# Summing the squares of two pairs with identity matmuls in PSUM, and leaving out the slope clamp

## The chip, the cores and the metric

The kernel runs on one core of one Trainium2 chip. The metric is the device time of one execution in microseconds, the median of several; before the change it was 736.23 us, the median of three runs from 736.1 to 736.62. The core has a matrix engine (TensorE, PE in the profile, with its weight loads shown apart as PEld), a vector engine (VectorE, DVE), an engine for functions of one input (ScalarE, ACT), a general engine (GpSimd, POOL) and a queue that issues transfers (SyncE, SP). Each runs its own instructions in the order in which they stand in its stream, and waits on semaphores for the others.

## What is computed

A linear attention with a complex, token-wise decay, then a dense layer pair with a softplus, then four experts with a ReLU. Only the attention's decay matters here:

```python
mag = np.sqrt(a_re * a_re + a_im * a_im)
scale = np.minimum(mag, 0.999) / (mag + 1e-06)
a_re_n, a_im_n = (a_re * scale, a_im * scale)
for t in range(S):
    ar, ai = (a_re_n[:, :, t, :, None], a_im_n[:, :, t, :, None])
    new_re = ar * S_re - ai * S_im
    new_im = ar * S_im + ai * S_re
    S_re, S_im = (new_re + kv, new_im)
    y[:, :, t] = np.einsum('bhd,bhde->bhe', q[:, :, t], S_re)
```

There are 2 batches, 8 heads, 768 tokens a batch and 48 numbers a head. The magnitude of the decay needs the sum of two squares, its logarithm and a running sum over the tokens; its angle needs an arctangent and a running sum as well.

## The kernel before

The tokens lie on the 128 partitions, 128 at a time (a chunk, 128 by 384 numbers for 8 heads). Two chunks make a pair; pairs 0 to 2 are batch 0, pairs 3 to 5 batch 1. For each pair `front(n)` makes the decay: `squares` (L545 to L547) squares both parts on ACT into T1 and T2 and adds them into T2, on DVE for pair 0 and on GpSimd for all others. `ratio` (L550 to L556) takes T1 to 1/|re| with a logarithm and an exponential on ACT, and four operations on DVE make the argument of the arctangent in `im`; the last of them, L556, clamps it to plus or minus 1.5. `logmag` turns T2 into the logarithm of the magnitude. `prefix` adds the last row of the chunk before (L574, on GpSimd, one partition) and makes the running sum by a matmul with a triangle of ones; `wrap`, `level` and `carry` copy it out and send the last row on by a transfer. `trig` takes sine and cosine. Sine and arctangent need another function table on ACT than logarithm and exponential, so `excursion` loads one table, runs them and loads the first again (L97). `back(n)` is the attention of the two chunks: `decay` (L653), the product with queries and keys QK (L665), transposes `tp` (L674), scores `sp` (L683) with the mask on DVE (L684), the mixing `yps` (L699), the state `sps` (L710), and X, the input of the dense layers, split in a high and a low half.

The dense layers of batch 0 (k = 0 and 1) run in the same stretch. Their weights arrive as 64-bit numbers in halves: three DVE operations (L70 to L72) join a half into one of two buffers `f`, ACT and DVE split it in two (L181, L182), and a transfer stores it for batch 1 (`moe_weights`). `gemm1` (L232) makes h; `first` and `second` make g from h by ACT and DVE (Abs, Exp, Ln, L250, L275, L276), and `third` (L314) multiplies g with the second weights into y. For k = 0 the tokens come in three blocks of two chunks, and one `e` or `g` holds two of the eight slices of the hidden layer: g_0_1, g_0_3, g_0_5 and g_0_7 are block 0.

The units of all these parts are put in one list of events with a place each, and sorted. From that list each engine's stream is laid down when the kernel is built: an instruction stands where the builder, which keeps its own account of when operands are ready, found it ready and first in the list. On the chip each stream is then run in that order. PSUM buffers of tag "a" (three) are shared by the running sums, the scores and the state.

Of the kernel before, what the change touches and what calls it, by code (L numbers as in the profile page):

```python
# [9 lines left out]
F32 = mybir.dt.float32  # L10
# [4 lines left out]
AF = mybir.ActivationFunctionType  # L15
ALU = mybir.AluOpType
# [7 lines left out]
P = 128  # L24
B, H, S, D = 2, 8, 768, 48
HD = H * D
# [23 lines left out]
SLOPE_MAX = 1.5  # L50
# [25 lines left out]
def fast_path(ctx: ExitStack, tc, bad, wsc, qkv, a_re, a_im, w_in, w_out, probs, w1, w2, out):  # L76
    nc = tc.nc
# [8 lines left out]
    psum = ctx.enter_context(tc.tile_pool(name="psum", bufs=1, space=PSUM))  # L86
# [6 lines left out]
    def behind(ins, earlier):  # L93
        tc.add_manual_dep(ins.ins, earlier.ins.name, NOSYNC, reason="order on one engine")
# [7 lines left out]
    def act(out_, in_, fn, **kw):  # L102
        i = nc.scalar.activation(out_, in_, fn, **kw)  # L103
        if fn in (AF.Exp, AF.Ln, AF.Sin, AF.Arctan):
            behind(i, tabs["load"])
            tabs["since"].append(i)
        return i

    use_table(LOGEXP)
    ident = const.tile([P, P], F32, name="ident")  # L110
# [12 lines left out]
    def column(name, value):  # L123
        t = const.tile([P, 1], F32, name=name)
        nc.vector.memset(t, value)
        return t
# [4 lines left out]
    b_tiny = column("b_tiny", 1e-37)  # L131
# [387 lines left out]
            third(*pipe.pop(0))  # L519

    rows = [None]
    st_S = [None]
    st = {}

# [3 lines left out]
    def wide(t, sl):  # L528
        return flat(t[:, sl, :])
# [13 lines left out]
    def squares(n, sl):  # L543
        R, I, T1, T2 = (wide(t, sl) for t in st[n])
        nc.scalar.activation(T1, R, AF.Square)  # L545
        nc.scalar.activation(T2, I, AF.Square)
        (nc.vector if n == 0 else nc.gpsimd).tensor_tensor(T2, T1, T2, ALU.add)  # L547

    def ratio(n, sl):
        R, I, T1, T2 = (wide(t, sl) for t in st[n])  # L550
        act(T1, T1, AF.Ln, bias=b_tiny)
        act(T1, T1, AF.Exp, scale=-0.5)
        nc.vector.tensor_tensor(R, R, T1, ALU.mult)
        nc.vector.scalar_tensor_tensor(R, R, 2.0, T1, ALU.subtract, ALU.mult)
        nc.vector.tensor_tensor(I, I, R, ALU.mult)
        nc.vector.tensor_scalar(I, I, SLOPE_MAX, -SLOPE_MAX, ALU.min, ALU.max)  # L556

    def logmag(n, sl):
        T1, T2 = wide(st["z0"][1] if n == 0 else st[n][2], sl), wide(st[n][3], sl)
        act(T2, T2, AF.Ln, bias=b_tiny)  # L560
        act(T1, T2, AF.Exp, scale=-0.5)
        nc.vector.tensor_scalar(T2, T2, 0.5, LOG_CAP, ALU.mult, ALU.min)
        nc.vector.scalar_tensor_tensor(T2, T1, -1e-6, T2, ALU.mult, ALU.add)
# [173 lines left out]
    def front(n):  # L737
        return [lambda: s1_load(n), lambda: squares(n, both), lambda: ratio(n, both), excursion(lambda: arctan(n)),
                lambda: logmag(n, both)] + s2_units(n) + [excursion(lambda: trig(n))]
# [40 lines left out]
    level(0, 0)  # L780
    decay(0, 0)
    squares(1, both)
    ratio(1, both)
    level(0, 1)
# [314 lines left out]
@with_exitstack  # L1099
def attention_moe_kernel(ctx: ExitStack, tc, qkv, a_re, a_im, w_in, w_out, probs, w1, w2, v, out):  # L1100
    nc = tc.nc
    top = ctx.enter_context(tc.tile_pool(name="top", bufs=1))
    bad = top.tile([1, 1], I32, name="bad")
    wsc = nc.dram_tensor("moe1_weights", (16, P, 768), F32).ap()
    fast_path(tc, bad, wsc, qkv, a_re, a_im, w_in, w_out, probs, w1, w2, out)
    xs = nc.dram_tensor("attention_out", (NTOK, HD), F32).ap()
    flag = nc.values_load(bad[0:1, 0:1], min_val=0, max_val=1)
    with tc.If(flag > 0):
        general_path(tc, xs, v, qkv, a_re, a_im, w_in, w_out, probs, w1, w2, out)
# [53 lines left out]
```

## Time and profile before

| What | Value |
|---|---|
| Median of three runs | 736.23 us |
| Profiled execution, its span | 736.2 us (nothing of its time is shown outside the span) |
| PE busy | 703.0 us, 95% |
| DVE busy | 584.7 us, 79% |
| ACT busy | 487.0 us, 66% |
| POOL busy | 33.3 us, 5% |
| Granted TensorE clock, mean | 0.986 |

The shares are means over stages that differ. In the 40 slices of the profile's page (18.4 us each) PE stands at 1, 6, 8, 8 and then 9 tenths throughout, while DVE is at 9 from the second to the eighth slice and lower later on. So the stages are read apart: the first 91 us, in which the attention of batch 0 and the weights' conversion fill DVE and ACT, and the rest, in which PE works without a pause.

### The profile page before, as it was taken

What the parts mean: (1) busy time and instruction counts of PE and PEld (TensorE: products, weight loads), DVE (VectorE), ACT (ScalarE), POOL (GpSimd) and SP (SyncE); (2) the same over time, 40 slices, a digit from 0 to 9 for tenths busy, and PEclk for the clock granted to TensorE, in tenths of its full rate; (3) what the DMA queues carried; (4) which work ended last, traced back from release to release, by engine and by line L of the source; (5) the groups of instructions that cost most, each with busy time, mean ns of one, the idle gap of its engine ahead of it and who ended that gap; (6) DMA issues with size and microseconds to landing.
All of it is one profiled execution on the core that took longest, in us unless ns stands there. A gap on an engine that the chain in (4) does not pass through costs nothing.

```text
span 736.2 us, 13313 instructions
## 1 busy us (share of the span) xinstructions
PE 703.0 (95%) x5171; PEld 676.2 (92%) x5171; DVE 584.7 (79%) x1150; ACT 487.0 (66%) x898; POOL 33.3 (5%) x31
## 2 busy tenths in 40 slices
PE   1688999999999999999999999999999999999996
PEld 0477899999899999999999999999999999999996
DVE  6999999955875854648888779988788899988963
ACT  7887886878896856345686666555556667666640
POOL 1132010000111011000000000000000000000000
PEclk9699999999999999999999999999999999999998
DMA  7655666721211420121022130213454445554501
GB/s 264 195 175 170 230 190 195 228 84 44 75 55 59 122 81 2 59 86 44 23 86 65 29 102 21 87 44 98 128 159 146 137 151 172 151 172 140 172 32 69
DMA packets 36486, 83.56 MB, mean 113 GB/s; under 512 B 4544, under 2 KB 13376, under 8 KB 36416
## 3 DMA queue, kind: packets, MB, share of 16 engines
q1 hardware_dynamic: 36128, 82.35, 35.5%
q8 instruction: 42, 0.69, 0.4%
q10 hardware_dynamic: 288, 0.30, 0.1%
q14 instruction: 28, 0.23, 0.1%
HBM read 73.95 MB, written 8.65 MB: 112 GB/s over the span
## 4 chain that ended last, share of the span: by engine, by line
PE 70%; DVE 10%; DMA 9%; ACT 8%; issue 2%; POOL 1%; SPq 0%; ACTq 0%; POOLq 0%; DVEq 0%
PE y L314 21%; PE h L232 18%; PE z L314 9%; PE px L425 7%; PE pv L425 3%; PE tp L674 2%; DMA rawB<-in_w_dram 2%; DMA chkw<-in_w_in_dram 2%; PE pc L425 2%; PE sp L683 2%; PE yps L699 2%; DMA chki<-in_a_im_dram 1%; PE ya L359 1%; PE sps L710 1%; DVE fA L72 1%
## 5 line engine op out<-in xcount | busy, mean ns | idle before, releaser
L232 PE MATMUL h<-X,A 128*128 128x384 f32 (+1 forms) x936 | 176.1, 329 | 2.5 <-ACT A L181 0.8
L232 PEld LDWEIGHTS h<-X,A 128*128 128x128 f32 x936 | 153.4, 188 | 5.8 <-issue 1.6
L314 PE MATMUL y<-B,g 128*128 128x384 f32 x744 | 150.0, 335 | 0.0
L314 PEld LDWEIGHTS y<-B,g 128*128 128x128 f32 x744 | 131.1, 188 | 0.5 <-issue 0.2
L314 PE MATMUL y<-g,B 128*128 128x384 f32 (+1 forms) x504 | 91.0, 315 | 0.3 <-ACT g L285 0.3
L314 PE MATMUL z<-B,g 128*128 128x384 f32 x372 | 84.7, 334 | 0.0
L314 PEld LDWEIGHTS y<-g,B 128*128 128x128 f32 x504 | 79.3, 189 | 1.9 <-ACT g L285 0.6
L314 PEld LDWEIGHTS z<-B,g 128*128 128x128 f32 x372 | 66.3, 188 | 0.0
L247 ACT ACTIVATE e<-h 128x384 f32<-128x384 f32 (+1 forms) x60 | 30.8, 513 | 37.3 <-PE h L232 36.3
L250 DVE SCALAR_TENSOR_TENSOR e<-h,e 128x384 f32<-128x384 f32 (+1 forms) x60 | 34.9, 581 | 21.0 <-ACT e L103 20.1
L255 DVE SCALAR_TENSOR_TENSOR g<-h,g 128x384 fp32r<-128x384 f32 x32 | 17.7, 554 | 28.2 <-ACT g L254 28.2
L103 ACT ACTIVATE e<-e,b_one 128x384 f32<-128x384 f32 (+1 forms) x60 | 38.2, 637 | 1.3
L103 ACT ACTIVATE e<-e 128x384 f32<-128x384 f32 (+1 forms) x60 | 32.8, 547 | 1.3
L425 PE MATMUL px<-X,sA 128*128 128x384 f32 x144 | 33.7, 339 | 0.0
L425 PE MATMUL px<-XC,sA 128*128 128x384 f32 x144 | 33.0, 337 | 0.1
L314 PE MATMUL z<-g,B 128*128 128x384 f32 x144 | 32.9, 335 | 0.0
L674 PE MATMUL tp<-ident,QK 128*96 128x128 f32 x192 | 27.3, 290 | 5.9 <-DVE QK L665 5.0
L674 PEld LDWEIGHTS tp<-ident,QK 128*96 128x96 f32 x192 | 22.4, 133 | 10.0 <-DVE QK L665 6.2
L254 ACT ACTIVATE g<-h 128x384 fp32r<-128x384 f32 x32 | 15.6, 487 | 21.3 <-PE h L232 21.1
L286 DVE TENSOR_TENSOR g<-e,g 128x384 fp32r<-128x384 f32 x48 | 26.7, 555 | 3.8 <-ACT g L285 3.0
L490 ACT CAST B<-rawB 128x768 fp32r<-128x768 f32 x24 | 20.0, 835 | 14.1 <-DMA rawB<-in_w_dram 7.6
L490 ACT CAST A<-rawA 128x384 fp32r<-128x384 f32 (+1 forms) x48 | 20.3, 457 | 11.6 <-DMA rawA<-in_w_dram 9.2
(204 smaller groups left out, 1424.4 us busy)
## 6 DMA issues: line engine op xcount, KB each, us to landing
rawA<-in_w_dram SPq DMA_DIRECT2D x32, 384.0 KB, 3.0
rawB<-in_w_dram SPq DMA_DIRECT2D x32, 384.0 KB, 3.1
rawA<-in_w_in_dram SPq DMA_DIRECT2D x16, 384.0 KB, 3.7
rawB<-in_w_out_dram SPq DMA_DIRECT2D x16, 384.0 KB, 3.8
chkw<-in_w_in_dram SPq DMA_DIRECT2D x16, 384.0 KB, 3.5
chkw<-in_w_out_dram SPq DMA_DIRECT2D x16, 384.0 KB, 3.3
qk<-in_qkv_dram SPq DMA_DIRECT2D x12, 384.0 KB, 3.3
v<-in_qkv_dram SPq DMA_DIRECT2D x12, 256.0 KB, 3.1
```

What stands on the lines that cost most here:

```text
L103: i = nc.scalar.activation(out_, in_, fn, **kw)
L232: nc.tensor.matmul(ps, wt[:, p, kk, o:o + P], XB[b][:, q, kk, tok], start=(n == 0), stop=(n == 3 * KT - 1))
L247: nc.scalar.activation(t, h, AF.Abs)
L250: nc.vector.scalar_tensor_tensor(t, h, 0.0, t, ALU.max, ALU.add)
L254: nc.scalar.activation(g[:, 0, :], h, AF.Relu)
L255: nc.vector.scalar_tensor_tensor(g[:, 1, :], h, 0.0, g[:, 0, :].bitcast(F32), ALU.max, ALU.subtract)
L286: nc.vector.tensor_tensor(g[:, 1, :], t, g[:, 0, :].bitcast(F32), ALU.subtract)
L314: mm = nc.tensor.matmul(ys[j], l_, r_, start=(opens and n == 0 and not mate), stop=(closes and n == 2), skip_group_check=k == 0)
L425: nc.tensor.matmul(ps, lt[:, p, li, :], rhs, start=(start and n == 0), stop=(stop and n == 2), skip_group_check=True)
L490: nc.scalar.copy(hi, src)
L674: nc.tensor.transpose(tp[:96, hh, :], src[:, hf * 4 + hh, :], ident)
L683: nc.tensor.matmul(sp[:, hh, :], kT[:, hh, :], qT[:, hh, :], start=True, stop=True)
```

## The change

The squares of pairs 1 and 2 are no longer added by GpSimd. For each chunk of these pairs two matmuls with the identity as weights add T1 and T2 into a PSUM buffer, and ACT takes the logarithm from there into T2, so that `logmag` doesn't take it any more. Pairs 0, 3, 4 and 5 add as before. The clamp L556 is left out for all six pairs.

```diff
+    ON_PE = (1, 2)
...
-        (nc.vector if n == 0 else nc.gpsimd).tensor_tensor(T2, T1, T2, ALU.add)
+        if n not in ON_PE:
+            (nc.vector if n == 0 else nc.gpsimd).tensor_tensor(T2, T1, T2, ALU.add)
+            return
+        for c in range(2):
+            ps = psum.tile([P, 512], F32, tag="a", name=f"sq{n}_{c}", bufs=3)[:, :HD]
+            nc.tensor.matmul(ps, ident, st[n][2][:, c, :], start=True, stop=False)
+            nc.tensor.matmul(ps, ident, st[n][3][:, c, :], start=False, stop=True)
+            act(st[n][3][:, c, :], ps, AF.Ln, bias=b_tiny)
...
-        nc.vector.tensor_scalar(I, I, SLOPE_MAX, -SLOPE_MAX, ALU.min, ALU.max)
...
-        act(T2, T2, AF.Ln, bias=b_tiny)
+        if n not in ON_PE:
+            act(T2, T2, AF.Ln, bias=b_tiny)
```

The builder lays the streams down anew, and they move far more than the diff tells. Three places follow, all between 35 and 60 us of the trace of before. The numbers behind the names count buffers and differ between the two kernels; lines after the change are 8 higher from `ratio` on.

On PE, the end of the attention of pair 0's second chunk and the first matmuls of the dense layers, before and then now (`sps_1` is the state of that chunk, `sq` the new sums, of pair 2):

```order
L699 MATMUL yps_1_397<-A_1_1_390,v_1_140 32x128 x2
L710 MATMUL sps_1_440<-v_1_140,QK_1_325 32x64 x11
L232 MATMUL h_0_0_548<-X_119,A_0_351 128x256 x2
L232 MATMUL h_0_2_677<-X_119,A_1_501 128x256 x2
L232 MATMUL h_0_0_548<-X_119,A_0_351 128x256 x16
```

```order
L707 MATMUL yps_1_400<-A_1_1_393,v_1_140 32x128 x2
L718 MATMUL sps_1_443<-v_1_140,QK_1_328 32x64 x24
L553 MATMUL sq_0_503<-t_490,ident 128x384
L554 MATMUL sq_0_503<-t_491,ident 128x384
L553 MATMUL sq_1_507<-t_490,ident 128x384
L554 MATMUL sq_1_507<-t_491,ident 128x384
L232 MATMUL h_0_0_557<-X_119,A_0_354 128x256 x18
```

The sums of pair 2 stand behind the last matmul of pair 0's attention.

On ACT, the table load of the excursion with pair 1's sine and pair 2's arctangent, before and now (t_487 and t_490 are T1 of pair 2, `dec` is the decay of pair 1, with which its attention begins):

```order
L675 COPY qT_1_0_337<-tp_1_0_338 96x512
L103 ACTIVATE t_487<-t_487,b_tiny 128x768
L103 ACTIVATE t_487<-t_487 128x768
L721 CAST X_119<-yps_0_279 128x3x128
L181 CAST A_1_501<-fA_1_0_506 128x384
L675 COPY kT_1_0_344<-tp_1_0_345 96x512
L675 COPY qT_1_1_356<-tp_1_1_357 96x512
L97 ACT_TABLE_LOAD
L675 COPY kT_1_1_363<-tp_1_1_364 96x512
```

```order
L181 CAST A_2_630<-fA_2_0_645 128x384
L103 ACTIVATE t_491<-sq_0_503,b_tiny 128x384
L103 ACTIVATE t_490<-t_490,b_tiny 128x768
L103 ACTIVATE t_491<-sq_1_507,b_tiny 128x384
L103 ACTIVATE t_490<-t_490 128x768
L97 ACT_TABLE_LOAD
L103 ACTIVATE re_129<-re_129,b_hpi 128x768
L103 ACTIVATE im_130<-im_130 128x768
L247 ACTIVATE e_0_1_625<-h_0_0_557 128x512
L103 ACTIVATE im_489<-im_489 128x768
L97 ACT_TABLE_LOAD
L103 ACTIVATE dec_0_541<-t_132 128x384 x2
```

Pair 2's logarithm and exponential moved from ahead of the work on pair 0's second chunk to behind its last step, the copy X, which is the row ahead of these, and the table load moved with them.

On DVE, the start of pair 1's attention (`qk`, `QK`), before and now:

```order
L72 SCALAR_TENSOR_TENSOR fB_1_1_579<-rawB_1_1_542,fB_1_1_579 128x384
L653 SCALAR_TENSOR_TENSOR qk_0_224<-dec_0_532,qk_0_224 128x768
L182 TENSOR_TENSOR B_1_539<-fB_1_0_558,B_1_539 128x384
L665 TENSOR_TENSOR QK_0_536<-qk_0_224,re_129 128x16x48
L665 TENSOR_TENSOR QK_0_536<-qk_0_224,im_130 128x16x48
```

```order
L72 SCALAR_TENSOR_TENSOR fB_2_0_787<-rawB_2_0_745,fB_2_0_787 128x384
L561 TENSOR_TENSOR re_488<-re_488,t_490 128x768
L562 SCALAR_TENSOR_TENSOR re_488<-re_488,t_490 128x768
L563 TENSOR_TENSOR im_489<-im_489,re_488 128x768
L661 SCALAR_TENSOR_TENSOR qk_0_227<-dec_0_541,qk_0_227 128x768
L673 TENSOR_TENSOR QK_0_545<-qk_0_227,re_129 128x16x48
```

The weights of A_2 and the first half of B_2 now stand ahead of pair 1's attention, and behind pair 2's `ratio` the next instruction is the one that waits for `dec`.

## Rows read from the trace of the kernel before

**Rows 1.** Waits of PE after 140 us: line, releaser, total us, times, longest
```profile
PE pf L586 <- ACT hl L580: 0.4, 1, 0.4
PE y L314 <- ACT g L285: 0.3, 1, 0.3
```

**Rows 2.** Stretches: length, busy us of PE, PEld, DVE, ACT, POOL, clock, DMA, GB/s
```profile
41.00:58.00 17.00, 13.56 (x184) 11.16 (x183) 16.97 (x29) 16.02 (x28) 2.32 (x2) 1.00 0.56 165
58.00:92.00 34.00, 31.68 (x406) 27.51 (x405) 32.16 (x60) 27.30 (x49) 5.93 (x4) 1.00 0.61 200
92.00:150.00 58.00, 58.00 (x584) 55.83 (x583) 55.09 (x110) 45.40 (x91) 2.44 (x1) 1.00 0.63 201
150.00:280.00 130.00, 129.21 (x1017) 123.79 (x1017) 83.60 (x134) 101.04 (x171) 13.84 (x11) 1.00 0.23 71
```

**Rows 3.** Chain that ended last, 88 to 96 us: start, us on it, what
```profile
90.83 0.52 ACT g L275
...
91.39 0.50 PE y L314 x2
```

**Rows 4.** Timeline, pair 1's sum: start, us, engine, line [idle before <- releaser]
```profile
12.09 0.89 PE L593 MATMUL pl<-t,tri 128*128 128x384 f32 x2
...
12.44 2.09 POOL L547 TENSOR_TENSOR t<-t,t 128x768 f32<-128x768 f32 x1 [10.71 <-ACT t L546]
12.91 2.04 DVE L555 TENSOR_TENSOR im<-im,re 128x384 f32<-128x384 f32 x1
...
14.57 0.94 ACT L103 ACTIVATE t<-t,b_tiny 128x768 f32<-128x768 f32 x1 [1.02 <-POOL t L547]
...
19.54 1.65 PE L593 MATMUL pf<-im,trik 128*128 128x384 f32 x2 [6.55 <-ACT im L103]
```

**Rows 5.** The clamp's line, all of the run: duration ns min/median/max
```profile
L556 DVE TENSOR_SCALAR im<-im x7: 349/550/555, 12.1 to 255.4; 128x768 f32<-128x768 f32 x5, 128x384 f32<-128x384 f32 x2
```

**Rows 6.** Timeline, 37 to 59 us: pair 2's sum and the excursion
```profile
37.36 1.82 POOL L547 TENSOR_TENSOR t<-t,t 128x768 f32<-128x768 f32 x1 [3.04 <-ACT t L546]
...
38.57 1.03 DVE L72 SCALAR_TENSOR_TENSOR fA<-rawA,fA 128x384 int32<-128x384 int32 x1
...
39.22 0.94 ACT L103 ACTIVATE t<-t,b_tiny 128x768 f32<-128x768 f32 x1 [1.47 <-POOL t L547]
...
40.19 0.85 ACT L103 ACTIVATE t<-t 128x768 f32<-128x768 f32 x1
...
40.63 0.99 POOL L574 TENSOR_TENSOR t<-rows,t 1x384 f32<-1x384 f32 x1 [0.17 <-DMA rows<-t]
...
47.62 0.68 DVE L684 TENSOR_TENSOR A<-sp,tri 128x512 f32<-128x512 f32 x1
...
48.29 0.94 ACT L103 ACTIVATE re<-re,b_hpi 128x768 f32<-128x768 f32 x1
48.36 0.86 PE L699 MATMUL yps<-A,v 128*32 128x128 f32 x24 [0.41 <-DVE A L684]
...
51.08 1.28 ACT L97 ACT_TABLE_LOAD   x1
...
52.38 0.94 ACT L103 ACTIVATE dec<-t 128x384 f32<-128x384 f32 x2
...
58.33 0.95 DVE L563 SCALAR_TENSOR_TENSOR t<-t,t 128x768 f32<-128x768 f32 x1
```

**Rows 7.** Timeline of DVE, 92 to 95 us: successive starts give the pitch
```profile
92.85 0.95 DVE L665 TENSOR_TENSOR QK<-qk,im 128x768 f32<-128x768 f32 x1
93.72 0.56 DVE L71 SCALAR_TENSOR_TENSOR fA<-rawA,fA 128x384 int32<-128x384 int32 x1
94.19 0.69 DVE L250 SCALAR_TENSOR_TENSOR e<-h,e 128x512 f32<-128x512 f32 x1
94.79 0.55 DVE L72 SCALAR_TENSOR_TENSOR fA<-rawA,fA 128x384 int32<-128x384 int32 x1
```

**Rows 8.** Timeline, pair 2's second wrapped angle, which the second excursion waits for
```profile
80.40 0.54 DVE L601 SCALAR_TENSOR_TENSOR im<-im,pf 128x384 f32<-128x384 f32 x1
```

## The prediction

> **What bounds the kernel now.** I read PE's waits first. After 140 us it waits for another engine in three places, 1.1 us in all, two of them in [rows 1]. Then the busy time by stretch: from 92 to 150 us PE is busy 58.00 of 58 us, from 150 to 280 us 129.21 of 130, while from 41 to 58 us it is busy only 13.56 of 17, and there DVE is busy 16.97 and ACT 16.02 [rows 2]. So the reader is to see two stages. Up to about 91 us DVE and ACT produce and PE waits on them; later PE alone sets the time, and an operation saved on DVE is worth nothing. The seam is in the chain of waits: ACT's cast of g_0_7 (L275) at 90.83 us is the last thing on the chain that isn't PE, and PE starts on g_0_7 at 91.39 [rows 3]. What the change is worth is how much earlier or later that point comes. The profiled execution has a span of 736.2 us and the median is 736.23, so the sum is made on the span.
>
> **What is removed.** *The clamp.* Seven instructions, 0.35 us for 384 columns and 0.55 for 768 [rows 5]. Two of the short and two of the long ones lie before 91 us. What they cost DVE is their pitch, about 0.3 and 0.47 (an instruction starts before the last one's record ends), but the two short ones overlap a wait of the same chain, so about 1.2 us. The three later ones run while PE is the bound: nothing.
>
> *Pair 1's sum on GpSimd* takes 2.09 us. DVE's multiplication L555 beside it starts at 12.91 and takes 2.04 us, where an operation of that size takes 0.55 [rows 4, 7]: about 1.5 us back. ACT's logarithm waited 1.02 us for it [rows 4]. *Pair 2's sum* takes 1.82 us; L72 beside it takes 1.03 instead of 0.55, so 0.5 us back, and ACT waited 1.47 us [rows 6]. Sum on DVE: 1.2 + 1.5 + 0.5 = 3.2 us.
>
> L555 ended 0.42 us after the GpSimd sum did, L72 likewise. The Trainium skill, SBUF — State Buffer, section Who interferes with whom, says that a DVE instruction with two SBUF inputs that comes second is blocked until the GpSimd one ends, whoever is first holding the port; both rows agree. By that rule alone a two-input instruction at the very start of pair 2's sum would give back up to 1.8 instead of 0.5 us; the row has 0.5, and I use that.
>
> **What is added.** *On PE* four matmuls of 128x384 for each pair, each in two passes that show as two records (0.89 us together at 12.09 us, 1.65 at 19.54 after a pause [rows 4]; by starts about 0.33 a pass when fast, an estimate): 2.6 us a pair. Pair 1's run right behind the fast row at 12.09 us, and PE then has nothing until 19.54: no cost to PE, and done near 15.3 us, where GpSimd was done at 14.53. At the slow row's rate they take about 5.1 us and pair 1 is late by 2.5; at best it gives back the 1.02 us that ACT waited. I take the fast rate, since nothing stands between. *On ACT* two logarithms of 384 columns instead of one of 768, an estimate from the 0.94 us row [rows 6] of 0.55 each, so 0.2 us more a pair. For pair 1 this leaves the first excursion about where it was.
>
> **What moves, and it is the largest term.** Pair 2's sums stand on PE behind pair 0's last state matmul, and pair 2's logarithm and exponential, which the table load must follow, stand on ACT behind pair 0's last X. In the kernel before, that exponential started at 40.19 us [rows 6]. Now it is walked from DVE's last mask of pair 0 (L684), 47.62 to 48.30 us before [rows 6]. With that logarithm, exponential and table load out of the way, ACT copies pair 0's transposes sooner, but the next matmuls wait for a row that GpSimd finishes near 41.6 us [rows 6]; I take the mask 2.1 us earlier, at 46.2 (bounds 0 and 3.2). From there: mixing 0.9 [rows 6], state 0.5, two of the four matmuls 1.3 and 0.2 until ACT sees them, logarithms 0.55, 0.85 and 0.5, exponential 0.85, table 1.28 [rows 6]: 6.9 us, so the cosine starts near 53.1 instead of 48.29. From cosine to the end of `dec` it is 52.38 + 0.94 - 48.29 = 5.0 us before [rows 6] and 5.1 to 5.3 now. `dec` is done at 58.4 instead of 53.3 us.
>
> DVE meets this in order. Its three operations of pair 2's `ratio` are done near 54.4 us (exponential at 51.8 plus 3 x 0.87), and the next one waits for `dec`: **a hole of 4 us**, behind which stand pair 1's QK, the first g and all weights that follow; no other work can fill it.
>
> Both kernels are then at the same clock time: 58.33 us in the one before, where DVE starts L563 of pair 2 [rows 6], and 58.4 now. What stands between that and the end of g_0_7's split on DVE differs. Now there is more: three QK steps of pair 1 and one of pair 2, 4 x 0.87; e_0_1 0.60; L562 0.47; two and three join steps of A_0 for the next layer, 0.94 and 1.24: 6.7 us. Less: two joins and a split of A_2's first half 1.41, three joins of its second 1.24, three of B_2's first 1.24: 3.9. Pitches are differences of starts: 0.87, 0.47 and 0.60 [rows 7]; the short L70 I put at 0.3. Net 2.8 us more. With the same waits and collisions as before in that stretch (DVE was busy 32.16 of 34 us [rows 2]), g_0_7 and with it PE's unbroken stretch come **2.9 us later: 736.2 + 2.9 = 739.1 us.**
>
> The same as a balance: savings -3.2, hole +4.0, work of the next layer put ahead of g_0_7 +3.0, smaller waits of before that the hole swallows -0.9. The 3.0 us are not lost on DVE, but after 91 us nobody pays for them. After that point PE has the same work, so nothing is given back.
>
> The Trainium skill, ScalarE: Activation LUTs, section What ACT_TABLE_LOAD costs, gives about 2.66 us for a switch of tables with its drain. Two switches now lie on the chain to `dec`, so by the page the hole would be longer by 2.7 us and the time 741.8. The rows have 1.28 us, and `dec` starts 0.02 us after the load's end [rows 6]; they decide.
>
> **Rivals.**
> *Faster.* The hole closes, because pair 2's sums run earlier than I walk them or DVE's queue is late enough to need those 4 us anyway. Then the savings stand: 736.2 - 3.2 = 733.0. It decides when `dec` ends before about 55 us. For it: DVE, not ACT, is the busier in [rows 2], and the mask may come up to 3.2 us earlier. Against: the table load waits for an exponential that waits for PE, in streams that can't pass each other.
> *No change.* The hole comes, but DVE runs from 58 us on without the 1.84 us that it idles there before [rows 2] and with fewer collisions with GpSimd: 2.9 less 2 to 3, so 736 to 737.
> *Slower still, by ACT.* The second excursion, with pair 2's sine, waits for the second wrapped angle on DVE, done at 80.94 before [rows 8], from which g_0_7's cast ended 10.4 us later. Now e_0_5 and two casts of A_0 come between, 13 us of ACT's work by my list, and the angle itself comes between 79.4 and 82.9: 92.4 to 96 instead of 91.35, so 737.3 to 740.8, and near 742 if both delays add.
>
> **How the numbers follow.** Forecast and the rival by ACT, slower by 1.6 to 6 us: 0.52. No change: 0.20. Faster by the savings: 0.28. Some 0.2%, 1.5 us, is what a measurement can tell from no change. The likeliest time is 739.1, its own range 737.3 to 742. As 0.28 is too much to leave out, the range for 8 in 10 reaches down to the savings, 732.8, and up to 742.0.
>
> **What would show it.** GpSimd has two sums fewer before 60 us, and L555 of pair 0 takes 0.55 us. The table load ahead of pair 1's cosine starts near 51.8 us and `dec` ends near 58.4; DVE is idle some 4 us before the first qk of pair 1, with ACT as what it waits for. A_2 is split about 8 us earlier than before. g_0_7's cast ends between 92 and 96 us, and from there on PE is busy as before. Wrong would be: the cast at or before 91 us; or PE waiting after 100 us.

## The result and the profile after

The changed kernel takes **746.26 us** (median of four runs, 745.71 to 748.77) against 736.42 us before (four runs, 736.1 to 736.8): a ratio of 1.0134, 95% interval 1.0114 to 1.0154. It is slower, as forecast, by more than three times the 2.9 us forecast, and above the range. Every run of it lasts 1.7 to 1.8 us longer than its span (the profiled one: 746.12 us, span 744.3), so spans are compared with spans here, and times with times: 744.3 less 736.2 is 8.1 us.

The stretches of [rows 2] in the changed kernel, the last two of before's 92 to 280 us as one row each (columns as there: length, busy us of PE, PEld, DVE, ACT, POOL, granted clock, DMA share, GB/s):

```profile
41.00:58.00 17.00, 14.68 (x194) 12.13 (x187) 14.68 (x29) 12.95 (x21) 0.00 (x0) 0.99 0.77 244
58.00:92.00 34.00, 26.92 (x362) 24.06 (x363) 30.72 (x52) 25.03 (x45) 7.13 (x5) 0.86 0.46 141
92.00:150.00 58.00, 55.94 (x585) 53.92 (x585) 52.62 (x101) 44.28 (x84) 3.27 (x1) 1.00 0.58 187
150.00:280.00 130.00, 128.97 (x977) 123.70 (x977) 85.77 (x136) 105.31 (x182) 11.91 (x9) 1.00 0.24 78
```

PE is idle for 7.08 us between 58 and 92 us, where it was idle for 2.32, its clock there is no longer whole, and it is idle for 2.06 us between 92 and 150, where it never was. DVE is idle for 3.28 us from 58 to 92 (1.84 before). What PE waits for from 58 to 150 us (line, releaser, total us, times, longest):

```profile
PE tp L682 <- DVE QK L673: 7.7, 1, 7.7
PE yps L707 <- DVE A L692: 1.2, 1, 1.2
PE pl L601 <- DVE A L692: 1.1, 1, 1.1
```

One wait carries it: pair 1's first transposes for its QK. The timeline of the changed kernel shows how it comes about (start, us, engine, line, operation; in brackets the idle time before it and what ended it). Lines from ratio on are 8 higher than before, so L563 stands for L555, L692 for L684, L661 and L673 for L653 and L665:

```profile
46.12 0.68 DVE L692 TENSOR_TENSOR A<-sp,tri 128x512 f32<-128x512 f32 x1
48.53 0.91 PE L553 MATMUL sq<-t,ident 128*128 128x384 f32 x2
50.18 0.58 ACT L103 ACTIVATE t<-sq,b_tiny 128x384 f32<-128x384 f32 x1 [0.85 <-PE sq L554]
52.08 0.83 ACT L103 ACTIVATE t<-t 128x768 f32<-128x768 f32 x1
52.92 1.28 ACT L97 ACT_TABLE_LOAD   x1
54.22 0.94 ACT L103 ACTIVATE re<-re,b_hpi 128x768 f32<-128x768 f32 x1
56.26 0.96 DVE L563 TENSOR_TENSOR im<-im,re 128x768 f32<-128x768 f32 x1
57.25 0.84 ACT L103 ACTIVATE im<-im 128x768 f32<-128x768 f32 x1 [0.88 <-DVE im L563]
59.40 0.94 ACT L103 ACTIVATE dec<-t 128x384 f32<-128x384 f32 x2
60.37 0.96 DVE L661 SCALAR_TENSOR_TENSOR qk<-dec,qk 128x768 f32<-128x768 f32 x1 [3.16 <-ACT dec L103]
63.34 3.62 PE L682 MATMUL tp<-ident,QK 128*96 128x128 f32 x16 [7.65 <-DVE QK L673]
```

Pair 0's last mask, pair 2's sums on PE, the logarithm, the exponential, the table load, the cosine, `dec`: the chain that the prediction walked, with `dec` done at 60.34 us instead of 53.32 [rows 6]. In [rows 6] the exponential started at 40.19 us, and its table load was done by 44.1; the cosine then waited for pair 1's own angle. The seam of [rows 3]:

```profile
85.00 0.54 DVE L609 SCALAR_TENSOR_TENSOR im<-im,pf 128x384 f32<-128x384 f32 x1
94.21 0.59 ACT L247 ACTIVATE e<-h 128x512 f32<-128x512 f32 x1
97.98 0.62 ACT L275 CAST g<-e 128x512 fp32r<-128x512 f32 x1
98.65 0.51 PE L314 MATMUL y<-g,B 128*128 128x256 f32 x2 [0.27 <-ACT g L275]
```

PE starts on g_0_7 at 98.65 us instead of 91.39 [rows 3], 7.3 us later. So far this is the forecast, only larger. The experiments show that the late `dec` is not the whole cause, and that the seam was the wrong place to read it.

### The profile page after: what moved, and what is told of

Its sections match the earlier page's. It is cut to its first block, busy times and chain, and to the rows that moved or that the text cites. A ratio compares the mean times of both kernels' runs of the same rounds, so it can differ in the third digit from the quotient of the medians.

```text
span 744.3 us, 13342 instructions
## 1 busy us (share of the span) xinstructions
PE 707.1 (95%) x5187; PEld 681.3 (92%) x5187; DVE 582.5 (78%) x1143; ACT 488.3 (66%) x900; POOL 29.8 (4%) x29
## 4 chain that ended last, share of the span: by engine, by line
PE 76%; DVE 10%; ACT 6%; DMA 3%; issue 2%; SPq 1%; POOL 0%; POOLq 0%; DVEq 0%; ACTq 0%
PE y L314 24%; PE h L232 16%; PE z L314 11%; PE px L425 10%; PE pv L425 5%; PE pc L425 3%; PE tp L682 2%; PE sp L691 2%; PE yps L707 2%; DVE QK L673 1%; ACT L97 1%; DMA rawA<-in_w_in_dram 1%; PE ya L359 1%; DVE qk L661 1%; DVE A L692 1%
## 5 line engine op out<-in xcount | busy, mean ns | idle before, releaser
L682 PE MATMUL tp<-ident,QK 128*96 128x128 f32 x192 | 28.9, 302 | 11.4 <-DVE QK L673 10.7
L682 PEld LDWEIGHTS tp<-ident,QK 128*96 128x96 f32 x192 | 23.9, 140 | 15.4 <-issue 8.3
L345 DVE SCALAR_TENSOR_TENSOR acc<-y,pr,acc 128x384 f32<-128x384 f32 x46 | 26.2, 610 | 1.7 <-PE y L314 1.7
```

What stands on the lines that cost most here:

```text
L345: nc.vector.scalar_tensor_tensor(dst, ys[j], pcol, dst, ALU.mult, ALU.add)
L682: nc.tensor.transpose(tp[:96, hh, :], src[:, hf * 4 + hh, :], ident)
```

## How the experiments are read

Two theories stood at the start. **O (order)**: pair 2's sums stand behind pair 0's last state matmul on PE, the table load waits for them, and that is the loss. **W (work)**: the added matmuls on PE, and what the builder lays anew around them, are the loss wherever anything waits for them. Rivals were C (the clamp's absence), P1 (pair 1's sums) and A (ACT's work ahead of g_0_7's cast).

Beside the time there is one point in the profile that all kernels pass with the same work still ahead, and after more than 150 us in which PE was 99% busy: ACT's cast of pair 5's first chunk into X. I call it **the marker**; all kernels have the same number of PE's instructions (2459) behind it. Of the kernel before, the changed one, and one with the clamp alone dropped:

```profile
318.53 0.48 ACT L721 CAST X<-yps 128x384 fp32r<-128x384 f32 x1 [2.27 <-PE yps L699]
```
```profile
327.71 0.48 ACT L729 CAST X<-yps 128x384 fp32r<-128x384 f32 x1 [2.27 <-PE yps L707]
```
```profile
318.64 0.48 ACT L729 CAST X<-yps 128x384 fp32r<-128x384 f32 x1 [2.27 <-PE yps L707]
```

The changed kernel is 9.2 us late at the marker. From the marker to the span's end the profiles take 415.7 to 418.4 us, whatever the kernel, the same kernel too (415.7 and 417.4), so a span or a single time tells nothing below 2 us. Ratios are of many runs on one chip against the kernel before there.

| kernel | ratio, 95% interval | marker, us later than before |
|---|---|---|
| changed | 1.0134, 1.0114 to 1.0154 | 9.2 |
| clamp alone dropped, two times | 0.9985, 0.9972 to 0.9998; 0.9995, 0.9979 to 1.001 | 1.0; 0.1 |
| pair 1's sums on PE, two times | 1.0020, 1.0002 to 1.0038; 1.0003, 0.9988 to 1.0018 | 0.3; -0.2 |
| pair 2's sums on PE | 1.0113, 1.0087 to 1.0139 | 9.5 |
| both on PE, clamp kept | 1.0154, 1.0138 to 1.017 | 11.9 |
| changed, pair 2 earlier | 1.0066, 1.0042 to 1.009 | 5.6 |
| changed, excursion split | 1.0068, 1.0047 to 1.0088 | 4.3 |
| changed, PE's gap filled | 1.0120, 1.0091 to 1.0149 | 7.8 |
| changed, second excursion later | 1.0199, 1.017 to 1.0229 | 16.3 |
| changed, no wait for the sums | 1.0057, 1.0037 to 1.0076 | 5.3 |
| clamp dropped, four unused matmuls at 49 us | 1.0070, 1.0051 to 1.0088 | 4.4 |
| the same at 65 us | 1.0065, 1.0038 to 1.0091 | 4.7 |
| the same at 105 us | 1.0049, 1.0035 to 1.0064 | 3.8 |
| twelve at 105 us | 1.0169, 1.0143 to 1.0196 | 10.0 |
| sums on DVE | 1.0048, 1.002 to 1.0076 | 1.0 |
| sums on GpSimd, own tile | 1.0002, 0.999 to 1.0013 | 0.5 |

## Which part of the change it is

**The clamp alone.**

```diff
-    ON_PE = (1, 2)
+    ON_PE = ()
```

> The slope clamp is dropped for every pair, all three sums of squares stay where they were in the kernel before (GpSimd for pairs 1 and 2). Theory O (order): what costs the time in the changed kernel is that pair 2's sums stand on PE behind pair 0's last state matmul, so that pair 1's second excursion and `dec` come about 7 us late. Here they are on GpSimd, so `dec` ends near 53 us and g_0_7's cast near 90: 735.0 us, 734.3 to 736.3. Rival C (the clamp's absence lets the builder shuffle the streams, and that costs): 738 us or more, with g_0_7's cast after 93 us.

Measured: 737.17 us, 0.9985, and once more with more runs:

> The kernel with the clamp alone dropped, once more with more runs, as the one that may beat both kernels: ratio to the kernel before 0.9985 in the first run with an interval just short of 1. If the two short and two long clamps before 92 us are worth the 1.2 us that the prediction gave them: 0.9985 again. If it is nothing: within 0.1% of 1.

Measured: 0.9995, interval 0.9979 to 1.001. Rival C falls. The two intervals overlap; the clamp's four instructions are worth between nothing and the 1.2 us of the prediction, and a measurement of this kernel can't tell which. The version doesn't beat the kernel before by anything that can be told.

**Pair 1's sums alone on PE** (`ON_PE = (1,)`).

> The clamp is dropped and pair 1's squares alone are summed on PE; pair 2's stay on GpSimd. Theory O (order): no hole, savings of 1.2 us (clamps) and 1.5 us (DVE's L555 no longer beside a GpSimd sum) stand: 733.5 us, 732.8 to 735.3, `dec` of pair 1's first half done near 53 us. Rival P1 (pair 1's sums on PE are what delays, by a late first excursion or by the matmuls at the slow clock): 738 us or more.

Measured: 739.23 us, 1.0020, the profile's marker within 0.3 us of before. The time lies in P1's range, the ratio between the theories, and the profiled run was the shortest of ten, so it was run again:

> The kernel with the clamp dropped and pair 1's sums alone on PE once more, since its runs spread over 6 us and its profiled one was the shortest. If pair 1's sums on PE cost time, the median stays 1.5 to 2.5 us above that of the clamp alone dropped, near 739; if they are free, as the prediction had it, it is within 1 us of 737.

Measured: 738.08 us, 1.0003. P1 falls as the cause of 1.3%: the two ratios stand 0.35% above the clamp alone dropped on the first chip and 0.08% in the second try, and both markers are within 0.3 us of before, so what pair 1's sums cost on PE is not told from zero with certainty, but it is small. They fill a pause of PE, as the prediction said. The savings of 2.7 us that theory O gave this kernel are not to be seen either.

**Pair 2's sums alone on PE** (`ON_PE = (2,)`).

> The clamp is dropped and pair 2's squares alone are summed on PE, behind pair 0's last state matmul as in the changed kernel; pair 1's stay on GpSimd. Theory O (order): the whole loss is here: 746 us, 744 to 748, DVE idle 3 us or more before pair 1's first qk, transposes of pair 1 at the lower clock. Rival P1 (pair 1's sums) or rival C (the clamp): not above the run with the clamp alone dropped, about 735.

Measured: 1.0113, 746.55 us, and the same three signs: `dec` ends at 60.63 us, DVE idle 3.16 us, PE idle 7.68 us between 58 and 92. Its interval and the changed kernel's overlap. So the loss is in pair 2's sums, as far as these intervals can tell (the marker is 9.5 us late, 9.2 in the changed kernel). That still leaves O and W open, since both the wait and the work are there.

**Both on PE, with the clamp kept.**

```diff
         nc.vector.tensor_tensor(I, I, R, ALU.mult)
+        nc.vector.tensor_scalar(I, I, SLOPE_MAX, -SLOPE_MAX, ALU.min, ALU.max)
```

> Both sums on PE as in the changed kernel, but the clamp stays for every pair. If the clamps cost what the prediction gave them, 1.2 us ahead of the late `dec`, and DVE waits there anyway, the hole swallows them: 745.5 to 747.5 us, as the changed kernel. If they count in full on DVE behind the hole: 747.5 or more. If the clamp's absence were what costs: below 742.

Measured: 749.51 us, 1.0154. The interval overlaps the changed kernel's; the marker is 2.7 us later than there, more than the 1.2 us that the clamps were given. The profile has another cause than the clamps: the builder put a cast of a weight half, which waits for DVE, on ACT ahead of pair 2's second logarithm.

```profile
52.25 0.51 ACT L181 CAST A<-fA 128x384 fp32r<-128x384 f32 x1 [2.01 <-DVE fA L72]
```

The table load starts at 54.82 instead of 52.92 us, `dec` ends at 62.56, and PE waits 11.09 us for QK. DVE has no hole there; weights fill it. So the order of the streams is another one, and this run doesn't show what the clamps cost behind the hole.

## Is it the wait or the work?

**Pair 2 earlier in the list.** Load, squares and ratio come right behind pair 0's second QK.

```diff
-    put([lambda: logmag(1, both)] + s2_units(1) + [lambda: s1_load(2), lambda: squares(2, both), lambda: ratio(2, both)]
-        + [excursion(lambda: trig(1), lambda: arctan(2))], -8, 0)
+    put([lambda: logmag(1, both)] + s2_units(1), -8, -2.9)
+    put([lambda: s1_load(2), lambda: squares(2, both), lambda: ratio(2, both)], -5.8, -5.7)
+    put([excursion(lambda: trig(1), lambda: arctan(2))], -0.73, 0)
```

> The changed kernel, with pair 2's load, squares and ratio put in the list right behind pair 0's second QK; PE's stream then has the four sums of pair 2 ahead of pair 0's last transposes instead of behind its last state matmul, and ACT's logarithms and exponential ahead of those transposes' copies. The operations are the same. Theory O (order): the excursion's table load no longer waits for pair 0's last matmul; `dec` ends near 54 us, no hole, savings stand in part: 734.5 us, 733 to 737. Rival W (the added work itself on PE and ACT, or the lower clock, wherever it stands): 740 us or more.

Measured: 743.31 us, 1.0066, in W's range. Half of the loss is gone, half stays. The sums start at 41.38 instead of 48.53 us, not at 37: on PE they still queue behind pair 0's first mixing and state. `dec` ends at 56.06, and PE still waits 2.43 us for QK.

**The excursion split.** Pair 1's sine and cosine no longer stand behind pair 2's exponential.

```diff
-    [..., lambda: s1_load(2), lambda: squares(2, both), lambda: ratio(2, both)]
-        + [excursion(lambda: trig(1), lambda: arctan(2))], -8, 0)
+    [..., lambda: s1_load(2), excursion(lambda: trig(1)), lambda: squares(2, both),
+         lambda: ratio(2, both), excursion(lambda: arctan(2))], -8, 0)
```

> The changed kernel, with pair 1's cosine and sine put into an excursion of their own ahead of pair 2's squares and ratio; pair 2's arctangent gets another excursion, so two table loads (2.6 us of ACT) are added. Pair 2's sums stay behind pair 0's last state matmul on PE. Theory O (order): pair 1's `dec` no longer waits for pair 2's exponential and ends near 52 us; DVE has no hole before pair 1's first qk, PE keeps its clock in its transposes, and g_0_7's cast ends near 92 to 94 us: 737 to 740. Rival W (the four added matmuls and split logarithms themselves delay PE and ACT in this stretch): 744 us or more. Rival A (ACT's 13 us between pair 2's second angle and g_0_7's cast set the end by themselves): the angle no earlier than 82, 743 to 746.

Measured: 741.67 us, 1.0068, between the theories. The wait is gone; the row of this kernel that shows it:

```profile
51.33 0.96 DVE L661 SCALAR_TENSOR_TENSOR qk<-dec,qk 128x768 f32<-128x768 f32 x1 [0.28 <-ACT dec L103]
```

DVE has no hole there, the clock is whole from 41 us on, and `dec` ends at 51.3 us, earlier than before. Yet 0.68% is lost. The two table loads that were added cloud this one: it could be they.

**No wait, and nothing else added.** ratio takes the logarithm of re^2 in place, over the squares that PE is still to read; that is why ACT waits for PE there at all. Given a tile of its own, and with the sums' logarithm moved to logmag behind the excursion, no table load waits for the sums, which stay on PE at the same place.

```diff
-            act(st[n][3][:, c, :], ps, AF.Ln, bias=b_tiny)
+            st["sq", n, c] = ps
...
-        act(T1, T1, AF.Ln, bias=b_tiny)
-        act(T1, T1, AF.Exp, scale=-0.5)
...
+        if n in (1, 2):
+            u = flat(att.tile([P, GM, HD], F32, tag="own", name=f"own{n}", bufs=1))
+        else:
+            u = T1
+        act(u, T1, AF.Ln, bias=b_tiny)
+        act(u, u, AF.Exp, scale=-0.5)
...
+        else:
+            for c in range(2):
+                act(st[n][3][:, c, :], st.pop(("sq", n, c)), AF.Ln, bias=b_tiny)
```

> The changed kernel with the same sums on PE at the same places. ratio writes the logarithm and exponential of re^2 to a tile of its own instead of over the squares that PE is to read, and the logarithm of the sums moves to logmag, behind the excursions. So no table load waits for PE's sums. Theory O (order by the wait): `dec` of pair 1 ends near 53 us, DVE has no hole, PE keeps its clock: 735 us, 733 to 738. Rival W (the work on PE and ACT): 742 us or more.

Measured: 742.17 us, 1.0057, in W's range. Theory O falls as the whole cause. The timeline has everything that it asked for, earlier than before [rows 6], and still the marker is 5.3 us late:

```profile
48.12 0.81 PE L554 MATMUL sq<-t,ident 128*128 128x384 f32 x2
48.24 1.28 ACT L97 ACT_TABLE_LOAD   x1
49.54 0.94 ACT L103 ACTIVATE dec<-t 128x384 f32<-128x384 f32 x2
52.62 0.95 DVE L680 TENSOR_TENSOR QK<-qk,re 128x768 f32<-128x768 f32 x1
...
91.05 1.47 PE L232 MATMUL h<-X,A 128*128 128x256 f32 x7 [3.37 <-DVE e L250]
```

The last row is one that the changed kernel doesn't have: near 91 us PE waits for DVE here, where with the clamp alone dropped it waits 0.2 to 0.3 us.

**The work without any use.** GpSimd sums as before (`ON_PE = ()`), without the clamp; at the place of pair 2's sums on PE stand four matmuls of the same kind on pair 1's old tiles, and nobody reads their result.

```diff
+    def spare_sums():
+        for c in range(2):
+            ps = psum.tile([P, 512], F32, tag="a", name=f"sq2_{c}", bufs=3)[:, :HD]
+            for i in range(2):
+                nc.tensor.matmul(ps, ident, st[1][2 + i][:, c, :], start=i == 0, stop=i == 1)
...
-    lambda: squares(2, both),
+    lambda: (squares(2, both), spare_sums()),
```

> The clamp is dropped and GpSimd makes the sums of pairs 1 and 2 as in the kernel before; four matmuls like those of pair 2's sums are added on PE at the place where the changed kernel has them, behind pair 0's last state matmul, reading pair 1's old tiles, and nobody uses their result. Theory O (order: what costs is that ACT's logarithm and exponential, and behind them the table load, wait for PE there): near the run with the clamp alone dropped, at most the matmuls' 2.6 us more: 736 to 739 us, `dec` of pair 1 ends before 54.5 us. Rival W (the added PE work at this place): 743 us or more.

Measured: 742.30 us, 1.0070, between the theories and near W. `dec` ends at 52.38 us, DVE idles 0.93 us ahead of pair 1's `qk`, nothing waits for the matmuls' result, and 0.7% is lost. They take 2.85 us, and what follows on PE:

```profile
49.16 2.85 PE L561 MATMUL sq<-t,ident 128*128 128x384 f32 x8
51.55 2.84 PE L232 MATMUL h<-X,A 128*128 128x256 f32 x20
55.72 1.49 PE L688 MATMUL tp<-ident,QK 128*96 128x128 f32 x12 [1.32 <-DVE QK L679]
```
```profile
50.71 4.80 PE L232 MATMUL h<-X,A 128*128 128x256 f32 x36 [0.95 <-ACT X L729]
56.25 1.93 PE L682 MATMUL tp<-ident,QK 128*96 128x128 f32 x16 [0.74 <-DVE QK L673]
```

The first three lines are of this kernel, the last two of the one with the clamp alone dropped (its second run). Pair 1's first transposes start no later than there, so up to that point the four matmuls have cost nothing; what they displaced comes behind. There the first two h of the layer run as one block of 36. Here the builder gave the block only 20 matmuls before pair 1's transposes and put 16 among and behind what follows them; ACT starts e_0_3 at 67.27 us instead of 60.17.

Four kernels have these matmuls on PE near their place and a `dec` that is done by 56.1 us, each by other means (earlier, split, no wait, unused). They lie between 1.0057 and 1.0070. Those with a `dec` between 59.7 and 60.7 us (changed, pair 2 alone, and one below with PE's gap filled) lie between 1.0113 and 1.0134. So both theories hold a part: by the middle values the work, with what the builder lays anew around it, costs 0.6 to 0.85% against the clamp alone dropped, and the wait another 0.4 to 0.8%.

## What 2.85 us of matmuls cost at other places

**The same four matmuls at two other places**, behind the first layer's first y (65 us) and ahead of pair 2's second transposes (105 us). In the first the block of 36 stays whole. The edit against the kernel just told, for the first place; the second has 12.0 for 3.0:

```diff
-    lambda: (squares(2, both), spare_sums()),
+    lambda: squares(2, both),
...
+    put([spare_sums], 3.0, 3.0)
```

> The same four matmuls that nobody uses, but behind the first layer's first y matmuls (near 65 us) instead of behind pair 0's last state matmul (near 49 us). Up to there PE's stream is that of the run with the clamp alone dropped: h_0_2 keeps its 18 matmuls together ahead of pair 1's transposes. Theory R (at 49 us the 2.9 us were the smaller part, and the larger one that h_0_2 was split behind pair 1's first chunk, which made e_0_3 7.6 us later): 739 to 740.5 us here. Theory W (the work on PE anywhere ahead of 92 us costs 5 to 6 us): 742 or more.

Measured: 742.58 us, 1.0065 (1.0038 to 1.0091). Theory R falls: with the block whole, ratio and marker (4.7 us late, 4.4 at 49 us) are no better, so splitting h_0_2 isn't what makes it dear.

> The clamp is dropped, GpSimd makes the sums of pairs 1 and 2, and the four matmuls that nobody uses stand late in PE's stream, ahead of the second transposes of pair 2 (near 105 us), where PE is nearly always busy. Theory T (time alone): what PE does more it ends later, 2.6 to 2.9 us on the run with the clamp alone dropped: 739.5 to 740.5. Theory P (an added stretch on PE there costs twice its length, because other engines' order is laid anew around it or the clock falls): 742 or more. Near 737: the stretch has slack that takes them in.

Measured: 741.28 us, 1.0049, 0.54 to 0.64% above the clamp alone dropped, 4 to 4.7 us by the ratios. By the marker it is 3.7 or 2.9 us, by which of the two runs of the clamp alone dropped it is set against. That lies between T and P and decides for neither.

**Three times as many there.**

```diff
-            for i in range(2):
-                nc.tensor.matmul(ps, ident, st[1][2 + i][:, c, :], start=i == 0, stop=i == 1)
+            for i in range(6):
+                nc.tensor.matmul(ps, ident, st[1][2 + i % 2][:, c, :], start=i == 0, stop=i == 5)
```

> Twelve instead of four matmuls that nobody uses, at the late place near 105 us, the clamp dropped and GpSimd making the sums. Four took 2.6 us there and cost 4.7 by the ratios. Theory T (PE's time counts once, and any new piece there costs about 2 us beside it, because the builder lays the streams anew): 737.2 + 7.8 + 2 = 747 us, 746 to 748. Theory P (PE's added time counts nearly twice): 737.2 + 14 = 751, 749 or more. Slack taken up by neither: 745 or less.

Measured: 749.27 us, 1.0169, 12.3 us above the clamp alone dropped on the same chip (737.0). By its times, then, added time on PE counts about one and a half times, 12.3 for 7.9, in P's range; but the ratio's interval alone reaches from 10.5 to 14.4 us above the kernel before. By the marker it counts little more than once: 9.9 or 9.0 us later than the two runs of the clamp alone dropped, and 6.2 us later than with four, for eight matmuls more, 5.2 us. PE's waits from 100 to 150 us with twelve, and with four:

```profile
PE yps L713 <- DVE A L698: 1.4, 1, 1.4
```
```profile
PE yps L713 <- DVE A L698: 0.8, 1, 0.8
PE y L314 <- ACT Y L326: 0.6, 1, 0.6
```

One of the two runs of the clamp alone dropped has none in that window, the other has the first of these too:

```profile
PE yps L707 <- DVE A L692: 1.0, 1, 1.0
```

So with the clamp alone dropped PE is idle for 0.08 or 1.12 us from 92 to 150, and 0.77 or 0.79 from 150 to 280 us; with four matmuls 1.68 and 0.95, with twelve 1.75 and 1.71. Work plus added waits is 2.7 + 1.8 = 4.5 us for four and 7.9 + 2.6 = 10.5 for twelve against the one run, 3.4 and 9.5 against the other; the markers stand 3.7 and 9.9 us behind that of the one, 2.9 and 9.0 behind that of the other. So at 105 us the work counts about once, and what comes beside it, up to 2 us, is not told from the scatter between two profiles of one kernel. The 2.4 us by which the times of twelve exceed the marker lie behind it, where profiles of one kernel differ by as much. That rest stays open.

At 49 and 65 us, where PE has pauses, the price at the marker is 3.5 to 4.6 us, no less than at 105. In both kernels PE waits 1.8 us for DVE's e near 91 us, where with the clamp alone dropped it waits 0.2 to 0.3: what the matmuls displace comes back as a wait for DVE. By which steps isn't shown. Nor is one rival tried: the unused sums also take two turns of the three PSUM buffers of tag "a", and the builder lays all streams anew around them; no run adds PE's time without these two.

## The clock, ACT, and two versions without PE

**PE's gap filled.** Nine unused matmuls that read pair 1's sines, in the 7.65 us in which PE waits.

```diff
+    def filler():
+        ps = psum.tile([P, 512], F32, tag="a", name="fill", bufs=3)[:, :HD]
+        for i in range(9):
+            nc.tensor.matmul(ps, ident, st[1][1][:, i % 2, :], start=True, stop=True)
...
+    put([filler], -0.7, -0.7)
```

> The changed kernel with nine matmuls of 128x384 added that read pair 1's sines once they are done (near 56 us) and whose result nobody uses, so that PE is not idle for 7.65 us ahead of pair 1's transposes; PE's order is otherwise the same up to 66 us. Theory K (the clock): the 16 transposes go back from 3.62 to about 2.0 us, the granted clock of 58 to 75 us back to 1.0, and the time falls by 2 to 3 us against the changed kernel, to about 743.5. Theory O (order): `dec` is as late as before, and the clock costs at most what DVE and ACT don't hide: 745 to 747 us.

Measured: 744.90 us, 1.0120. The first two lines are of the changed kernel, the next two of this one (columns as in [rows 2]), and the last is this one's transposes:

```profile
56.00:63.00 7.00, 0.00 (x0) 0.00 (x0) 3.77 (x5) 6.09 (x11) 0.98 (x1) 0.61 0.31 102
63.00:68.00 5.00, 4.66 (x23) 4.54 (x24) 5.00 (x8) 5.00 (x11) 1.38 (x1) 0.52 0.27 82
```
```profile
56.00:63.00 7.00, 6.39 (x21) 3.66 (x22) 3.81 (x5) 6.90 (x13) 0.99 (x1) 1.00 0.25 79
63.00:68.00 5.00, 5.00 (x85) 4.73 (x87) 4.86 (x9) 5.00 (x10) 1.65 (x1) 1.00 0.26 79
```
```profile
62.68 1.96 PE L682 MATMUL tp<-ident,QK 128*96 128x128 f32 x16 [0.42 <-DVE QK L673]
```

After PE has stood still, its granted clock is near half, 1.2 instead of 2.4 GHz, and 16 transposes take 3.62 us; kept busy, it has the whole clock and they take 1.96 us. The marker moves by 1.3 us. The ratio moves by 0.14%, 1 us, which the intervals don't tell from nothing. The clock is a part, and a small one.

**The second excursion later.** e_0_7 stands ahead of it on ACT.

```diff
-    put([lambda: logmag(2, both)] + s2_units(2) + [excursion(lambda: trig(2))], 1.3, 7.5)
+    put([lambda: logmag(2, both)] + s2_units(2), 1.3, 6.7)
+    put([excursion(lambda: trig(2))], 8.2, 8.25)
```

> The changed kernel, with pair 2's sine and cosine put later in the list, so that e_0_7 stands ahead of that excursion's table load on ACT and g_0_7's cast right behind it. Everything up to 85 us is the same, the late `dec` and the idle stretch of PE too. Rival A (ACT's work between pair 2's second angle and g_0_7's cast sets the end): g_0_7's cast ends 4 to 6 us earlier, near 93.5, and the time falls to 741 to 743 us, as far as pair 2's QK, now later, doesn't give it back near 107 us. Theory O (order) with DVE as what carries the delay: within 1 us of the changed kernel, 745.3 to 747.

Measured: 752.75 us, 1.0199, outside both forecasts, and this is the run I learned most from. ACT now has time ahead of e_0_7, and g_0_7's cast comes no earlier (97.58 instead of 97.98 us):

```profile
91.90 1.24 PE L232 MATMUL h<-X,A 128*128 128x256 f32 x9
93.40 0.51 ACT L181 CAST A<-fA 128x384 fp32r<-128x384 f32 x1 [2.86 <-DVE fA L72]
93.82 0.59 ACT L247 ACTIVATE e<-h 128x512 f32<-128x512 f32 x1
96.28 1.28 ACT L97 ACT_TABLE_LOAD   x1
97.58 0.62 ACT L275 CAST g<-e 128x512 fp32r<-128x512 f32 x1
```

Rival A falls. With ACT's work taken away e_0_7 starts only 0.39 us earlier (93.82 instead of 94.21): the h that it reads ends on PE at 93.14 us, the first of these rows, and the cast ahead of it waits for DVE until 93.40. From 84.27 to 97.38 us the changed kernel's PE waits for nobody. PE had become the bound by 84 us, because it was behind, and the seam at 98 us is where PE's own backlog ends. Putting the excursion later made pair 2's `dec` 6.4 us later (101.08 instead of 94.70), and PE is idle for 6.17 us from 92 to 150 instead of 2.06, most of it in waits for g, for QK and its transposed copy, and for a mask.

**The sums on DVE**, neither on GpSimd nor on PE, and **on GpSimd with a tile of its own** for ratio's logarithm, so that ACT doesn't wait for them. Both have `ON_PE = ()`.

```diff
-            (nc.vector if n == 0 else nc.gpsimd).tensor_tensor(T2, T1, T2, ALU.add)
+            (nc.vector if n in (0, 1, 2) else nc.gpsimd).tensor_tensor(T2, T1, T2, ALU.add)
```

> The clamp is dropped for every pair and the sums of squares of pairs 1 and 2 are made by DVE, neither by GpSimd nor by PE: two additions of 128x768 more on DVE. Theory O (order): a DVE addition of 0.95 us replaces the 1.5 and 0.5 us by which DVE was held beside GpSimd's sums, and ACT's logarithms don't wait 1.0 and 1.5 us: 735 us, 733.5 to 736.5, no slower than with the clamp alone dropped. Rival D (DVE is the bound in this stretch, so 1.9 us more work on it count in full): 737 us or more.

Measured: 739.54 us, 1.0048 (1.002 to 1.0076). Rival D by its times: two additions of 0.95 us on DVE cost more than the 2.0 us by which DVE was held beside GpSimd's sums. Its marker, 1.0 us late, doesn't show the loss, so its place stays open.

The second has the tile `u` of the kernel without a wait.

> The clamp is dropped, GpSimd makes the sums of pairs 1 and 2 as in the kernel before, and ratio's logarithm has a tile of its own, so ACT's logarithm doesn't wait for GpSimd's sums (1.02 and 1.47 us before). Theory O: the excursions come 1 to 1.5 us earlier than with the clamp alone dropped; as DVE is nearly full in this stretch, the time gains at most that: 734 to 737 us. Rival: a GpSimd sum meets other two-input operations of DVE instead, no gain or a loss: 737 to 739.

Measured: 737.59 us, 1.0002. No gain. No version here beats the kernel before by anything that came twice.

## Why the prediction was right and wrong, point by point

**What bounds the kernel: wrong, and this is the step that failed.** "Up to about 91 us DVE and ACT produce and PE waits on them" was taken from the chain and from 41 to 58 us. But [rows 2] also has PE busy 31.68 of 34 us from 58 to 92, only 0.48 us less than DVE. In that stretch DVE and PE are both nearly full and hand work to each other. So the prediction gave pair 2's matmuls no price on PE, and carried the hole to the end from DVE's balance alone. What the runs showed in its place: four matmuls on PE whose result nobody uses make the marker 3.5 to 4.3 us later, and the late `dec`, with PE waiting for it, another 3.6 to 4.9 us where 2.9 were forecast.

**Span taken for time.** The prediction set before's span, 736.2 us, equal to its median. With the 1.7 to 1.8 us around a span in every run since, that execution was presumably about 1.7 us longer than the median one. So 8.1 of the 9.8 us are to be looked for between the two profiles.

**Pair 1's sums: right.** They ran from 12.47 us in PE's pause, and without GpSimd's sum beside it pair 0's L563 took 0.56 instead of 2.04 us [rows 4]:

```profile
11.86 0.56 DVE L563 TENSOR_TENSOR im<-im,re 128x384 f32<-128x384 f32 x1
...
12.47 1.19 PE L553 MATMUL sq<-t,ident 128*128 128x384 f32 x2
```

Their savings, 1.5 us on DVE, are not to be seen at the end, though, and the clamp's hardly.

**Pair 2's 2.6 us on PE: mis-sized.** The matmuls' length was right (2.85 us from the first to the last end), but the sum has 1.3 us of them, inside the chain to `dec`, and nothing for PE itself. The unused matmuls put its price, against the clamp alone dropped, at 3.5 to 4.3 us at the marker (322.95 against 319.49 and 318.64) and at 0.75 to 0.85% of the time, 5.5 to 6.3 us. That is some 40 to 60% of the loss, 9.2 us at the marker and 9.8 by time, and no rival had it.

**The moved excursion: right in kind.** The mask was walked to end at 46.2 us and ended at 46.80. The table load was walked to 51.8 and came at 52.92: 0.6 us of that is the mask's and 0.3 the mixing's and the state's. From cosine to the end of `dec` it took 6.1 us instead of the 5.1 to 5.3 of the walk, because pair 2's arctangent, which shares the excursion, waited 0.88 us for DVE's L563. So `dec` came at 60.34, not 58.4.

**The hole on DVE: right** (4 us forecast, 3.16 measured). **What it does to the end: wrong.** 2.9 us were carried over to the end from DVE's balance alone. PE idled 7.65 us around that hole and lost 1.7 us on the transposes at the lower clock, and behind it PE was the bound (above), so that DVE's balance no longer told the end. The wait's price, from the kernels with and without it: 3.6 to 4.9 us at the marker (9.2 less the 4.3 to 5.6 of the four without the late `dec`), of which the clock 1.3.

**"After that point PE has the same work, so nothing is given back": half right.** It has the same work, but from 92 to 150 us it is idle for 2.06 us, where it never was: 1.17 for a mask, 0.62 for DVE's e and 0.27 for g_0_7. PE waiting after 100 us was among the signs of being wrong.

**The rival by ACT: its number came true and its mechanism did not.** It named 13 us from the second wrapped angle to g_0_7's cast; the profile has 13.06 (85.54 to 98.60). The run that took ACT's work away left the cast where it was, within 0.4 us. **Faster**: the hole did not close; it needed a `dec` before about 55 us, and the kernels with these matmuls that have one are slower all the same. **No change**: DVE was to make good 2 to 3 us behind the hole. Of its 3.28 us of idle time from 58 to 92 us, 2.37 are the hole's, so behind it 0.91 are left of 1.84, and 0.9 us was made good.

**Table loads: right.** The row has 1.28 us and the cosine 0.02 us behind its end, as in [rows 6]. The Trainium skill (ScalarE: Activation LUTs, What ACT_TABLE_LOAD costs) has the same 1.28 us for the load itself, but 2.66 us for every switch with a drain; no run here shows that drain as time behind the load.

Summed up at the marker, in us: the wait 3.6 to 4.9, the work with what is laid anew around it 3.5 to 4.3, the clamp and pair 1's sums -0.2 to 1.0; 9.2 was measured. How 2.85 us of work become 3.5 to 4.3 stays open.

## What to carry to other kernels

Before an operation is moved to an engine that "waits anyway", read that engine's idle time in that stretch and in the one behind it. Here PE idled for 3.44 of 17 us at the place itself and was 93% busy in the 34 us behind it, and a move of 2.85 us cost more than its length. Test a suspected wait and a suspected cost apart, with the work left in and its result unused, and with the wait taken out and the work left in; one of the two alone would have shown only half of the loss here. And a forecast number that comes true doesn't show its mechanism: take that mechanism away and see whether the time moves.

## What the runs showed of the hardware

PE's clock reacts to a single wait in an otherwise busy stage: after 7.65 us of standing still the granted clock was 0.52 over the next 5 us. With pair 2 earlier, where PE stood still for 2.43 us, the 16 transposes took 2.85 us, between the 1.96 of the filled gap and the 3.62.

GpSimd's addition of a single row of 384 elements takes 1.38 us and holds a DVE operation of full width beside it from 0.96 to 1.76 us:

```profile
65.67 1.38 POOL L582 TENSOR_TENSOR t<-rows,t 1x384 f32<-1x384 f32 x1 [6.52 <-DVE t L571]
66.12 1.76 DVE L661 SCALAR_TENSOR_TENSOR qk<-dec,qk 128x768 f32<-128x768 f32 x1
```

The Trainium skill (SBUF — State Buffer, Who interferes with whom) has it that the instruction that comes second waits until the other has ended; the row ends 0.83 us behind GpSimd's, about the pitch of such an operation alone (0.87 in [rows 7]), and agrees. That GpSimd works on one partition only doesn't help: DVE is held by 0.8 us here, between the 0.5 and the 1.5 us of the sums over 128 partitions [rows 4, 6].
